# One of three shifted bit patterns on GpSimd, query rows and turned products by DMA, features by fours, in a one-core gated attention kernel

## The chip, the cores and the metric

The kernel runs on one core of a Trainium2 chip. The metric is the device time of one execution in microseconds (us); the median of the runs shown is the time of a version. A core has TensorE (PE in the profile, its weight loads are PEld), VectorE (DVE), ScalarE (ACT), GpSimd (POOL) and SyncE (SP, which here only issues DMAs). Each engine works through its own instructions in order and waits on semaphores.

## What is computed

Two attention blocks over the same x, mixed by a gate. S = 2048 rows, D = 512, 32 heads of 16.

```
x = A_x                                   # (1, 2048, 512) bfloat16
g = sigmoid((x * gate_w).sum(-1))
# A: softmax attention
q, k, v = split(x @ A_wqkv)               # 32 heads of 16
p = softmax(q k^T / 4);  a = (p v) @ A_wo
# B: linear attention with learned features
q, k, v = split(x @ B_wqkv)
phi(t) = [softmax(t w_phi), softmax(-t w_phi)]        # 32 features a head
o = phi(q) (phi(k)^T v) / (phi(q) sum(phi(k)) + 1e-6);  b = o @ B_wo
out = g * a + (1 - g) * b
```

## The kernel before, in words

**Branch A.** The queries go in four chunks of 512 columns, and in each the 32 heads as eight groups of four heads: 32 groups. A group takes 16 key tiles of 128 rows. One key tile of one group is a *pack*; there are 512 packs, and a pack has four *units* (one head, 128 keys, 512 queries). For a unit TensorE makes the scores in a row of 32 of its array (`_scores`, L814), an engine makes the exponential, and TensorE multiplies it with the values in a column of 32 (`_values`, L928), four heads side by side, adding up over the 16 key tiles in one PSUM bank of the group. A column of ones in the values gives the denominators.

Two engines make exponentials. *ScalarE* (`_exp`, L862) takes three units and two units in turn out of a ring of five PSUM banks. *VectorE* takes the packs that the table `AWAY` (L713) marks, 109 in all, at most five of a group's key tiles 1, 4, 7, 10, 13. It makes a linear bit pattern out of the scores (`_vector_bits`, L755, one operation for each unit, PSUM to SBUF, uint16), which read as bfloat16 is an exponential with straight lines between powers of two, and then three copies shifted by a constant (`_vector_terms`, L771, `SHIFTS`, up to two packs in one operation). TensorE adds all four patterns up by multiplying each with the values, two of them with values scaled by 0.75 (`vc`). So such a pack has 16 value matmuls and not 4.

`_norm` (L944) ends a group: a transpose in blocks of 32 from PSUM (n_t1, L949), the denominators times the gate's factor (n_den), a reciprocal (n_rec), a product (n_mul, L960), and for each second group a transpose back (n_back, L965), into `onTA`, from which the output matmuls read. `_proj_q` (L637) makes the queries of two groups: a projection, and one VectorE operation (L651) that writes them twice, times a mask, so that in each copy the other group's rows of 16 are zero.

**Branch B.** `_b_pair` (L1056) works on two tiles of 128 rows: a projection to the features' arguments (pq, L1069), its negative beside it (b_neg, L1086), a tree of maxima (b_max), the subtraction (b_sub, L1091), the exponential on ScalarE (b_exp, L1094), a tree of sums, reciprocals and products (`_b_scale`). Three slots of `bq` hold such pairs. For the keys `_b_kv` (L1125) multiplies the features with the values and adds the result to `kvacc` on VectorE; for the queries `_b_phit` turns them by a transposing DMA, and `_b_num` (L1182) makes the numerators, the denominators (nb_den, L1200), a reciprocal and a product (nb_mul, L1204). `_b_out` and `_out` multiply with the output weights, B and A into the same bank.

**The order.** Nothing is ordered by hand within an engine. Every operation is given to a planner (`Plan`) with an engine, a cost, its dependencies, a priority in packs ("due") and sometimes an earliest pack (`rel`). `Plan.order` goes through time and takes for each engine what is ready, the most urgent first; `emit` writes out one queue for each engine and the semaphores. Three PSUM banks beside the ring are given out as they come free. So that TensorE keeps busy, the planner sets filler matmuls by zero weights between (`_fill`, L935) and full matmuls ahead of scores (L835). Constants of `_Kernel` (L363 to L369, and L968) move whole kinds of operations: `BITS`, `STEP`, `LEAD`, `TERM`, `NORM`, `QDUE`, and `K0`, `SK`, `Q0`, `SQ` for branch B. All but a few DMAs are issued by SP, in planned order.

Of the kernel before, what the change touches and what calls it, by code (L numbers as in the profile page):

```python
# [10 lines left out]
P = 128  # L11
# [32 lines left out]
class Op:  # L44
    def __init__(self, eng, fn, cost, name, prio, rel, kind, lat):
# [17 lines left out]
        self.filled = 0  # L63

# [38 lines left out]
class Plan:  # L103
# [9 lines left out]

    def __init__(self):
        self.ops = []
        self.now = -1
        self.free_banks = []
        self.keep = None
        self.open = None
        self.pad = None  # L120

    def op(self, eng, fn, cost, reads=(), writes=(), deps=(), name="", prio=0.0, rel=-99, kind="full",
# [24 lines left out]
        o.array = cost if array is None else array  # L147
        self.ops.append(o)
# [7 lines left out]
    def order(self):  # L156
# [5 lines left out]
        for o in self.ops:  # L162
            if not o.left:
                avail[o.eng].append(o)
        free = dict.fromkeys(self.ENGS, 0.0)
# [5 lines left out]
        while left:  # L171
            best = None
            for e in self.ENGS:
                found, limit = [], 1e9
                for o in avail[e]:
# [8 lines left out]
                    if o.acquire is not None:  # L184
                        banks = self._bank_for(o)
                        if not banks:
                            continue
                        r = min(b[1] for b in banks)
                        if r > t:
                            t = r  # L190
                    o.ready = t
# [51 lines left out]
            free[e] = array.seq if e == "PE" else o.end  # L243
            queues[e].append(o)
# [113 lines left out]
class _Kernel:  # L358
# [5 lines left out]
    NB, LEAD = 4, 15.75  # L364
    FIRST = 13
    KT0, KTS, NKT = 1, 3, 5
    KEEP = 14
    TURN = 2.5
    STEP, BITS, TERM, PVX, NORM, QDUE, PUT = 0.55, -40.0, 4.0, -0.4, -6.0, -15.5, 8  # L369
# [28 lines left out]
    def _memory(self, ctx):  # L398
# [31 lines left out]
        self.qT = sb("qT", [P, self.NQS, QCH], BF16)  # L430
        self.ET = sb("ET", [P, self.NSLOT, QCH], BF16)
        self.T1 = sb("T1", [P, 2, 16, 32], F32)
        self.rinv = sb("rinv", [P, 2, 16], F32)
        self.T2 = sb("T2", [P, 16, 32], BF16)
        self.ghb = sb("ghb", [P, self.NT], F32)
# [4 lines left out]
        self.bq = sb("bq", [P, 3, 2, 2 * D], BF16)  # L440
        self.btree = sb("btree", [P, 32, 8, 4], BF16)
        self.bsum = sb("bsum", [P, P], F32)
        self.brec = sb("brec", [P, P], FP16)
# [8 lines left out]
        self.warm = self.bq[:, 2, 0, 0:QCH]  # L452
        self.wpp = self.bq[:, 2, 1, 0:4 * P].rearrange("p (c j) -> p c j", c=4)
        self.gwb = self.bq[:, 2, 0, QCH:2 * QCH].rearrange("p (c m) -> p c m", c=4)
# [107 lines left out]
    def _projections(self):  # L562
# [5 lines left out]
        self.b_onTA = [[B() for _ in range(4)] for _ in range(2)]  # L568
        self.b_T1, self.b_rinv, self.b_T2 = [B(), B()], B(), B()
        self._warm(9)  # L570
        for j in range(NQC):
            if j == 0:
                self._proj_k0(0, 2)
                self._proj_q(0, 0, 3)
                self._proj_k0(1, 4)
            else:
                self._proj_k(0, j)
# [51 lines left out]
    def _proj_k(self, cp, j):  # L629
        due = 32 * cp + 3 * j - 14.0 if cp else 4 * j - 2.0  # L630
# [6 lines left out]
    def _proj_q(self, qc, cp, bank=None):  # L637
        n = qc * 4 + cp
        due = 32 * n + self.QDUE if n else -2.0
# [3 lines left out]
        reads = [self.b_xT[qc], self.b_WA[0][cp > 0], self.b_mask]  # L643
        if n == 0:
            one = lambda side: lambda e, b: e.tensor_scalar(self.qT[:, s0 + side, :], b, self.mask[:, side:side + 1],
                                                            None, op0=ALU.mult)
            self._proj(lhs, rhs, reads, [one(0), one(1)], self.c_dve(512), due, due - 99, "qproj",
                       [self.b_qT[s0], self.b_qT[s0 + 1]], bank=bank)
            return
        self._proj(lhs, rhs, reads,  # L650
                   [lambda e, b: e.tensor_tensor(self.qT[:, s0:s0 + 2, :], b[:, None, :].to_broadcast([P, 2, QCH]),  # L651
                                                 self.mask[:, :, None].to_broadcast([P, 2, QCH]), ALU.mult)],
                   self.c_dve(1024), due, due - 10, "qproj", [self.b_qT[s0]])
        self.b_qT[s0 + 1] = self.b_qT[s0]

    def _proj_v(self, cp, j):
# [3 lines left out]
        due = 32 * cp + 4 * j - (6.5 if cp else 0.5)  # L660
# [15 lines left out]
    def _gate(self):  # L676
# [4 lines left out]
        z = self.bq[:, 0:2].rearrange("p s t j -> p (s t j)").bitcast(F32).rearrange("p (q b d) -> p q b d", q=NQC, d=32)  # L681
        for qc in range(NQC):
            job = Job()

            def mm(e, qc=qc, job=job):
# [4 lines left out]
            m = op("PE", mm, 4 * self.c_pe(512), reads=[self.b_xT[qc], b_gwb], name="gate", prio=18 + qc, rel=12,  # L690
                   acquire=job)
            last.append(op("DVE", lambda e, qc=qc, job=job: e.transpose(
                z[:, qc].rearrange("p b d -> p (b d)"), self._bank(job)), 0.74, deps=[m], name="gate_t", prio=18 + qc,
# [3 lines left out]
        for r, sign in ((0, -1.0), (1, 1.0)):  # L697
# [3 lines left out]
        self.gate_z = last[-2:]  # L701
# [5 lines left out]
        self.b_ghb.writers = [op("DVE", lambda e, i=i: e.tensor_copy(  # L707
            self.ghb[32 * i:32 * i + 32, :],
            self.gh[32 * i:32 * i + 32, 1].rearrange("p q (t i) -> p (q t) i", i=4)[:, :, i]), 0.1, reads=[self.b_g],
            name="gate_b", prio=26) for i in range(4)]  # L710


    AWAY = (4, 5, 23, 20, 5, 27, 30, 14, 27, 22, 15, 25, 13, 30, 7, 31, 27, 31, 18, 21, 23, 26, 27, 29, 15, 29, 11, 25, 15, 26, 29, 15)  # L713

    def _plan_vector(self):
# [16 lines left out]
        for n in range(1, 4 * self.NQC):  # L732
            self.hooks.setdefault(max(0, 32 * n - 30), []).insert(0, lambda n=n: self._proj_q(*divmod(n, 4)))
# [8 lines left out]
    def _vector_bits(self, pair, side, pack, due):  # L742

        op = self.plan.op
        tile, b = self.va[:, pair, side], self.b_va[pair][side]
        step = self.STEP
        parts = []
        for j in range(self.NB):
# [7 lines left out]
                tile[:, j, :], self._bank(job), SCALE * LOG2E * 128.0, (127.0 - LOG2_SUM) * 128.0,  # L756
                op0=ALU.mult, op1=ALU.add), self.c_dve(512), deps=[m] + b.readers, name="v_bits", prio=at + self.BITS,
                release=job))
        b.writers, b.readers = parts, []
        self.last_bits = parts  # L760

    def _vector_terms(self, pair, packs):
# [3 lines left out]
        for j, pack in enumerate(packs):  # L766
            self.terms[pack] = [(self.va[:, pair, j], self.b_va[pair][j], 0)]
        a, n = flat(self.va[:, pair]), size * self.NB * QCH
        for k, (shift, scaled) in enumerate(SHIFTS):
            t, b = self.vp[:, k], self.b_vp[k]  # L770
            self.plan.op("DVE", lambda e, t=t, shift=shift: e.tensor_scalar(flat(t), a, float(shift), None, op0=ALU.add),  # L771
                         0.07 + n * 0.00026, reads=self.b_va[pair][0:size], writes=[b], name="v_term",
                         prio=packs[0] + self.TERM)
            for j, pack in enumerate(packs):
                self.terms[pack].append((t[:, j], b, scaled))

    def _attention(self):
# [12 lines left out]
        self.b_va, self.b_vp = [[Buf(), Buf()] for _ in range(2)], [Buf() for _ in SHIFTS]  # L790
        self._value_copies()
# [78 lines left out]
    def _pv(self, p):  # L870
# [10 lines left out]
        for u in range(4 * p, 4 * p + 4):  # L881
            deps.append(self.exps[self.in_group[self.place[u]]])
            src[u % 4] = self.ET[:, self.place[u] % self.NSLOT, :]
# [26 lines left out]
    def _pv_terms(self, p):  # L910
# [3 lines left out]
        for tile, buf, scaled in self.terms.pop(p):  # L914
            src = {i: tile[:, i, :].bitcast(BF16) for i in range(4)}
            V = self.vc[:, g8 // 2, (kt - self.KT0) // self.KTS] if scaled else None
# [7 lines left out]
    def _values(self, e, ot, g8, kt, src, V=None):  # L924
        V = self.V[:, kt, g8 // 2] if V is None else V
        for i, tile in src.items():
            v0 = 17 * (2 * i + g8 % 2)
            ins = e.matmul(self._bank(ot)[32 * i:32 * i + 32, :], V[:, v0:v0 + 32], tile,  # L928
# [15 lines left out]
    def _norm(self, qc, src, side, last, dst, b_dst, due, job, alone=False):  # L944
# [19 lines left out]
        if side == 1:  # L964
            op("DVE", lambda e: e.transpose(dst, T2[:].rearrange("p b s -> p (b s)")), 0.63,  # L965
               reads=[b_T2], writes=[b_dst], name="n_back", prio=due)

    K0, SK, Q0, SQ = 28.0, 11.85, 206.0, 16.8  # L968

    def _branch_b(self):  # L970
        op, NT, NQC = self.plan.op, self.NT, self.NQC
        B = Buf
        self.b_bq = [B() for _ in range(3)]
        for b in self.b_bq[:2]:
            b.readers = list(self.gate_z)
        self.b_WT = B()
        self.b_WP = [B() for _ in range(2)]
        self.b_tree, self.b_bsum, self.b_brec = B(), B(), B()
# [6 lines left out]
        self.n_pair = 0  # L985
# [4 lines left out]
        self.b_bq[2].readers = self.b_gwb.readers + self.b_warm.readers + self.b_wphi.readers  # L990
        for t in range(0, NT, 2):
            due = self.K0 + self.SK * t
            self._b_v(t, due)
            self._b_v(t + 1, due + 1)
# [316 lines left out]
```

## Time and profile before

| | before |
|---|---|
| median of 3 runs (lowest to highest) | 780.46 us (779.11 to 780.57) |
| profiled execution, its own time | 787.43 us |
| its span, first to last instruction | 785.5 us |
| mean granted TensorE clock in it | 0.987 |
| exponentials of scores (L862), count | 645 |
| feature exponentials (L1094), count and mean | 16, 2027 ns |
| bit operations of VectorE (L755), count | 436 |
| issues on SP: transposing DMAs of features and of branch B's products | 16 and 16, 3.2 and 2.4 us to landing |

A row of the groups of instructions has the line, the engine, the operation, output and inputs with their shapes, the count, and then the busy time in us, the mean of one in ns, and how long the engine was idle just before such instructions and who ended it. VectorE's and ScalarE's records of neighbouring instructions overlap a little, so means times counts add up to more than busy time. A row of the waits has the waiting engine and line, the one that released it, the total in us, the times, and the longest.

### The profile page before, as it was taken

How to read it: one execution, taken by the hardware profiler on the slowest of the kernel's cores; microseconds unless marked ns; L12 is line 12 of the kernel's file. 1: busy time of each engine (PE TensorE's matmuls, PEld its weight loads, DVE VectorE, ACT ScalarE, POOL GpSimd, SP SyncE). 2: the span in 40 equal slices, each digit the busy share in tenths (PEclk: the TensorE clock that was granted, in tenths of full speed). 3: DMA queues.
4: the chain of work that ended last, by engine and by line, in shares of the span. 5: the costliest groups of instructions: out<-in, count | busy, mean ns of one | idle time of the engine just before them, and what ended most of it. 6: DMA issues, size and time to landing. Idle time of an engine off the chain costs nothing.

```text
span 785.5 us, 16524 instructions
## 1 busy us (share of the span) xinstructions
PE 753.5 (96%) x7224; PEld 234.9 (30%) x7294; DVE 713.1 (91%) x1178; ACT 762.1 (97%) x665; POOL 6.4 (1%) x16
## 2 busy tenths in 40 slices
PE   9999999999999999999999999999999999999998
PEld 3333333233212222222222232223222222222222
DVE  3779999998969999999999997998999999988994
ACT  6999999999969999999999999999999999999996
POOL 2000000000000000000000000000000000000000
PEclk9999999999959999999999999999999999999999
DMA  9200000000000000000101020010200102001010
GB/s 223 100 3 1 2 1 2 1 1 2 1 1 2 1 2 1 1 2 1 29 1 28 8 41 21 9 34 15 41 8 8 41 2 55 8 8 41 8 22 28
DMA packets 42183, 15.75 MB, mean 20 GB/s; under 512 B 36992, under 2 KB 41600, under 8 KB 42112
## 3 DMA queue, kind: packets, MB, share of 16 engines
q1 hardware_dynamic: 40240, 14.05, 8.1%
q8 instruction: 57, 0.93, 0.5%
q10 hardware_dynamic: 1872, 0.66, 0.4%
q14 instruction: 14, 0.11, 0.0%
HBM read 4.21 MB, written 2.10 MB: 8 GB/s over the span
## 4 chain that ended last, share of the span: by engine, by line
ACT 61%; PE 21%; DVE 16%; issue 1%; DMA 1%
ACT ET L862 59%; PE ps L814 7%; DVE va L755 7%; PE ps L928 6%; DVE vp L771 4%; PE ps L611 3%; ACT bq L1094 2%; PE ps L935 1%; PE ps L1221 1%; PE ps L665 1%; DMA xT<-in_A_x_dram 1%; PE ps L1254 1%; DVE T L949 1%; PE ps L835 1%; DVE bq L1069 0%
## 5 line engine op out<-in xcount | busy, mean ns | idle before, releaser
L862 ACT ACTIVATE ET<-ps 128x1536 bf16<-128x1536 f32 (+1 forms) x645 | 734.6, 1349 | 14.1 <-PE ps L814 13.2
L814 PE MATMUL ps<-qT,kT 32*128 32x512 bf16 x2048 | 342.0, 387 | 14.7 <-ACT ET L862 5.7
L755 DVE TENSOR_SCALAR va<-ps 128x512 uint16<-128x512 f32 x436 | 283.1, 680 | 18.0 <-PE ps L814 17.3
L771 DVE TENSOR_SCALAR vp<-va 128x4096 uint16<-128x4096 uint16 (+1 forms) x183 | 199.6, 1101 | 1.7 <-PE ps L928 1.2
L814 PEld LDWEIGHTS ps<-qT,kT 32*128 32x128 bf16 x2048 | 84.9, 91 | 276.4 <-ACT ET L862 153.0
L928 PE MATMUL ps<-ET,V 128*32 128x512 bf16 x1612 | 155.9, 390 | 0.3 <-DVE nb L1204 0.3
L928 PE MATMUL ps<-vp,vc 128*32 128x512 bf16 x872 | 75.8, 384 | 0.5 <-DVE vp L771 0.3
L935 PE MATMUL ps<-kT,zero 128*32 128x512 bf16 x784 | 70.9, 390 | 0.0
L928 PEld LDWEIGHTS ps<-ET,V 128*32 128x32 bf16 x1612 | 40.7, 95 | 69.7 <-issue 56.4
L611 PE MATMUL ps<-WB,xT 128*128 128x512 bf16 x167 | 50.6, 393 | 3.9 <-issue 2.4
L928 PE MATMUL ps<-va,V 128*32 128x512 bf16 x436 | 43.7, 391 | 0.0
L928 PE MATMUL ps<-vp,V 128*32 128x512 bf16 x436 | 42.2, 389 | 0.5 <-DVE vp L771 0.4
L611 PE MATMUL ps<-xT,WA 128*128 128x512 bf16 (+1 forms) x117 | 33.8, 381 | 2.4 <-issue 2.1
L1094 ACT ACTIVATE bq<-bq 128x2048 bf16<-128x2048 bf16 x16 | 32.4, 2027 | 0.0
L949 DVE STREAM_TRANSPOSE T<-ps 128x512 f32<-128x512 f32 x32 | 22.7, 710 | 7.8 <-PE ps L928 7.7
L928 PEld LDWEIGHTS ps<-vp,vc 128*32 128x32 bf16 x872 | 19.9, 95 | 31.9 <-issue 18.4
L1069 DVE CAST bq<-ps 128x512 bf16<-128x512 f32 x32 | 21.8, 683 | 5.8 <-PE ps L611 5.7
L935 PEld LDWEIGHTS ps<-kT,zero 128*32 128x32 bf16 x784 | 17.3, 94 | 31.9 <-issue 29.6
L665 PE MATMUL ps<-WA,xT 128*128 128x128 bf16 x256 | 20.6, 220 | 0.3 <-DVE WB L1043 0.3
L611 PEld LDWEIGHTS ps<-WB,xT 128*128 128x128 bf16 x192 | 13.0, 99 | 22.8 <-issue 13.2
L1091 DVE TENSOR_TENSOR bq<-bq,btree 128x2048 bf16<-128x2048 bf16 x16 | 19.4, 1215 | 0.1
L651 DVE TENSOR_TENSOR qT<-ps,mask 128x1024 bf16<-128x1024 f32 x15 | 18.2, 1212 | 1.4 <-PE ps L611 1.4
(80 smaller groups left out, 376.2 us busy)
## 6 DMA issues: line engine op xcount, KB each, us to landing
WB<-in_B_wqkv_dram SPq DMA_DIRECT2D x1, 1536.0 KB, 7.4
out_dram<-WB SPq DMA_DIRECT2D x12, 128.0 KB, 1.7
WA<-in_A_wqkv_dram SPq DMA_DIRECT2D x3, 384.0 KB, 4.9
WoA<-in_A_wo_dram SPq DMA_DIRECT2D x1, 512.0 KB, 8.4
WoB<-in_B_wo_dram SPq DMA_DIRECT2D x1, 512.0 KB, 9.0
WA<-in_A_wqkv_dram ACTq DMA_DIRECT2D x3, 128.0 KB, 4.1
phiT<-bq SPq DMA_TRANSPOSE x16, 3.2
WT<-nb SPq DMA_TRANSPOSE x16, 2.4
```

Of the source, the lines that this page charges most:

```text
L611: ins = e.matmul(self._bank(job)[:, 0:n], lhs(c), rhs(c), start=(c == 0), stop=(c == 3))
L665: ins = e.matmul(self._bank(job)[:, P * tt:P * tt + P], self.xT[:, c, QCH * j + TOK * tt:QCH * j + TOK * tt + TOK], self.WA[:, 2, c, P * c ...
L755: parts.append(op("DVE", lambda e, j=j, job=job: e.tensor_scalar(tile[:, j, :], self._bank(job), SCALE * LOG2E * 128.0, (127.0 - LOG2_SUM) ...
L771: self.plan.op("DVE", lambda e, t=t, shift=shift: e.tensor_scalar(flat(t), a, float(shift), None, op0=ALU.add), 0.07 + n * 0.00026, reads= ...
L814: return e.matmul(out, self.kT[32 * i:32 * i + 32, cp, kt * TOK:(kt + 1) * TOK], self.qT[32 * i:32 * i + 32, s, :], start=True, stop=True, ...
L862: o = plan.op("ACT", lambda e: e.activation(self.ET[:, a % NS:a % NS + n, :], self.ps[:, self._ring(a):self._ring(a) + n, :], ACT.Exp, sca ...
L928: ins = e.matmul(self._bank(ot)[32 * i:32 * i + 32, :], V[:, v0:v0 + 32], tile, start=(kt == 0), stop=(kt == self.NT - 1), tile_position=( ...
L935: ins = e.matmul(self._bank(ot)[32 * i:32 * i + 32, :], self.zero[:], self.kT[:, 0, 0:QCH], start=False, stop=False, tile_position=(0, 32 ...
L949: op("DVE", lambda e: e.transpose(T1[:, side].rearrange("p b s -> p (b s)"), src()), 0.635, deps=last, writes=[b_T1[side]], name="n_t1", p ...
L1069: [lambda e, b, k=k: e.tensor_copy(bq[:, k].rearrange("p (g s v) -> p g s v", g=8, s=2)[:, :, 0, :], b.rearrange("p (g v) -> p g v", g=8))],
L1091: + [("b_sub", two(2048), lambda e: e.tensor_tensor(x, x, spread(tree[:, :, 0]), ALU.subtract))],
L1094: op("ACT", lambda e: e.activation(flat, flat, ACT.Exp), self.c_act(2048) + 0.045, reads=[b], writes=[b], name="b_exp", prio=due + 1)
```

## The change, and its diff

- **Shifted patterns.** The first of the three (`BY_POOL = 0`) is made by GpSimd, one pack at a time. Such an operation, a *rider*, is bound to the first bit operation of the next pack: it waits for VectorE's operation just ahead of it in VectorE's queue, so that it runs beside the four bit operations. The planner keeps GpSimd's riders and VectorE's operations named in `SHARED` apart in time.
- **Packs.** `AWAY` marks 111 packs, other ones than before; many constants of the order move, `BITS`, `BURST` (for `STEP` within a pack) and `FIRST` among them.
- **Query rows.** VectorE copies the projection once (`qs`), and eight DMAs on SP put rows of 16 into the two copies of `qT`, whose other rows GpSimd clears at the start. The very first queries are projected in two halves of 256 columns and written by VectorE as before (`_proj_q0`).
- **Turned products.** n_back becomes 16 DMAs that place blocks of 32 by 32 (`turned`) and one transposing DMA, except for the last pair of groups.
- **Features by fours.** `_b_quad` takes four tiles; the negative is not made: maxima and minima are taken of the same argument, two subtractions write two sides, and ScalarE's exponential has the scale +1 or -1. Sums, reciprocals and products go over four tiles at once. `bq` holds one such set in place of three pairs. `kvacc` is added to once for four tiles.
- **Numerators.** The gate's factor goes from a product with the denominators into one fused operation (scalar_tensor_tensor).

The diff, cut to its core:

```diff
-    NB, LEAD = 4, 15.75
-    FIRST = 13
+    NB, LEAD = 4, 16.0
+    BURST, RIDE = 0.1, 2.5
+    FIRST = 5
-    KEEP = 14
+    KEEP = 13
+    GAP, KDUE, VDUE, GATE = 3.45, -16.25, -11.75, 14.0
-    STEP, BITS, TERM, PVX, NORM, QDUE, PUT = 0.55, -40.0, 4.0, -0.4, -6.0, -15.5, 8
+    BY_POOL = 0
+    STEP, BITS, TERM, PVX, NORM, QDUE, PUT = 0.625, -80, 5.5, 0.8, 2, -22.0, 3.8
...
-    K0, SK, Q0, SQ = 28.0, 11.85, 206.0, 16.8
+    K0, SK, Q0, SQ = 33.0, 12.25, 216.0, 16.0
...
+    SHARED = {"v_term", "b_max", "b_sub", "b_sum", "b_rec", "b_ratio", "b_mul", "n_den", "n_rec", "n_mul", "n_back",
+              "kvbd", "vcopy", "gate_h", "gate_b", "gate_z"}
...
+                    if o.port:
+                        t = max(t, port[other[e]])
...
+            for x in o.riders:
+
+                x.deps.extend(queues[e][-1:])
...
+    def _rider(self, eng="POOL"):
...
+        (pair, side, pack), k = self.riding, self.BY_POOL
+        shift, scaled = SHIFTS[k]
+        self.riding = None
+        b = self.b_vp[k][side]
+        o = self.plan.op(eng, lambda e: e.tensor_scalar(
+            self.vp[:, k, side], self.va[:, pair, side], float(shift), None, op0=ALU.add),
+            self.RIDE if eng == "POOL" else 0.07 + self.NB * QCH * 0.00026, reads=[self.b_va[pair][side]], writes=[b],
+            name="v_term", prio=pack + self.TERM)
+        o.port = True
...
         for k, (shift, scaled) in enumerate(SHIFTS):
...
+            if k == self.BY_POOL:
+                continue
...
+        tile = self.qs[:, n % 2]
+        self._proj(lhs, rhs, reads, [lambda e, b: e.tensor_copy(tile, b)], self.c_dve(512), due, due - 10, "qproj",
+                   [self.b_qs[n % 2]])
+        parts = [lambda e, r=r: e.dma_start(self.qT[r:r + DH, s0 + r // DH % 2, :], tile[r:r + DH, :])
+                 for r in range(0, P, DH)]
...
-        if side == 1:
+        if side == 1 and alone:
             op("DVE", lambda e: e.transpose(dst, T2[:].rearrange("p b s -> p (b s)")), 0.63,
                reads=[b_T2], writes=[b_dst], name="n_back", prio=due)
...
+        elif side == 1:
+            parts = [lambda e, i=i, x=x: e.dma_start(self.turned[32 * x:32 * x + 32, :, 32 * i:32 * i + 32],
+                                                     T2[32 * i:32 * i + 32, x:16:4, :])
+                     for i in range(4) for x in range(4)]
+            self.dma("SP", f"on{due:.0f}", parts, cost=0.55 * len(parts), reads=[b_T2], writes=[self.b_turned], prio=due,
+                     lat=3.0)
...
+        for side, out, alu in ((1, n, ALU.min), (0, p, ALU.max)):
+            t, buf = self.btree[:, side], (pos, neg)[side]
+            at = 6 - 2 * side
+            fold("b_max", 32, t, p, alu, at, [pos], tree[side])
+            run("b_sub", two(2048), lambda e, out=out, t=t: e.tensor_tensor(out, p, spread(t[:, :, 0], 32), ALU.subtract),
+                at, [pos, tree[side]], [buf])
+            op("ACT", lambda e, side=side: e.activation(sides[side], sides[side], ACT.Exp, scale=1.0 - 2 * side),
+               self.c_act(2048) + 0.045, reads=[buf], writes=[buf], name="b_exp", prio=due + gap * at + 1)
...
+            op("DVE", lambda e, hf=hf, sums=sums: e.reciprocal(rb[:, hf], sums()[:, :, 16]), 0.17,
+               deps=[m] + b_nb.writers, writes=[b_rb], name="nb_rec", prio=due)
+            parts.append(op("DVE", lambda e, hf=hf, sums=sums: e.scalar_tensor_tensor(
+                out=nb[:, 256 * hf:256 * hf + 256].rearrange("p (h d) -> p h d", d=16), in0=sums()[:, :, 0:16],
+                scalar=self.ghb[:, t:t + 1], in1=rb[:, hf, :, None].to_broadcast([P, 16, 16]), op0=ALU.mult,
```

## The prediction, made before the changed kernel had run

> **What bounds the kernel now.** I read the busy table first, then ScalarE's waits, then both ends of the timeline, then VectorE by form, then GpSimd.
>
> From the page, busy time, share of the span and instructions:
>
> ```profile
> PE 753.5 (96%) x7224; PEld 234.9 (30%) x7294; DVE 713.1 (91%) x1178; ACT 762.1 (97%) x665; POOL 6.4 (1%) x16
> ```
>
> Two engines are above 90% beside TensorE, whose busy figure is stretched by pipelining and by filler matmuls (L935, 784 of them). ScalarE is idle for only 785.5 - 762.1 = 23.4 us. Its whole list of waits, as total, times, longest:
>
> ```profile
> ACT ET L862 <- PE ps L814: 13.2, 7, 5.5
> ACT xT L1260 <- PE ps L1254: 4.2, 1, 4.2
> ACT L862 <- issue: 2.3, 1, 2.3
> ACT ET L862 <- PE ps L928: 0.3, 1, 0.3
> ```
>
> Two of them are the start (5.5 and 2.3), one is the end (4.2, and about 2.7 us more pass after its last instruction). Six waits of L814 remain, 13.2 - 5.5 = 7.7 us. Windows (PE, PEld, DVE, ACT, POOL busy, then the granted clock, DMA) put them in one place:
>
> ```profile
> 196.00:220.00 24.00, 22.38 (x204) 6.40 (x199) 22.36 (x36) 22.63 (x20) 0.00 (x0) 0.90 0.01 2
> 220.00:240.00 20.00, 19.67 (x117) 4.05 (x114) 13.57 (x24) 13.54 (x11) 0.00 (x0) 0.61 0.00 0
> 240.00:300.00 60.00, 57.63 (x599) 16.76 (x600) 58.08 (x88) 59.93 (x54) 0.00 (x0) 1.00 0.01 1
> 300.00:400.00 100.00, 96.25 (x934) 28.30 (x947) 99.88 (x164) 99.88 (x87) 0.00 (x0) 1.00 0.03 7
> ```
>
> From about 215 to 235 us TensorE had half its clock; outside that stretch ScalarE is never idle for long. The profiled execution took 787.43 us (span 785.5 and 1.93 around it). Without the 7.7 us it is 779.7; the runs shown lie at 779.11 to 780.57, median 780.46. So I take it that the timed runs had no such stretch, and that between its first exponential at 9.08 us and its last, which ends at 777.5, **ScalarE sets the time**. VectorE is full as well at 300 to 400 us, but ScalarE was not waiting for it there.
>
> **The change, part by part.**
>
> *Two more packs on VectorE (109 to 111).* ScalarE loses 8 of 1612 score units. The chain of waits has 50 exponentials in 56.51 us and 47 in 53.34, so one of three units and one of two take 2 x 1.13 = 2.26 us, 0.45 per unit: 8 x 0.45 = **-3.6 us on the path**. The feature exponentials stay sixteen of 2048 columns, with runs of 64 instead of one block; between nothing and the 0.1 us by which these sixteen differ among themselves, each, I take nothing. TensorE gets 24 more value matmuls, six sets of four at 0.22 us, 1.3 us, and VectorE 8 more bit operations. TensorE has cover: its score weight loads waited 153.0 us for ScalarE.
>
> *One of three shifted patterns to GpSimd.* The rows that VectorE shows:
>
> ```profile
> L755 DVE TENSOR_SCALAR va<-ps 128x512 uint16<-128x512 f32 x436 | 283.1, 680 | 18.0 <-PE ps L814 17.3
> L771 DVE TENSOR_SCALAR vp<-va 128x4096 uint16<-128x4096 uint16 x144 | 173.5, 1214 | 1.6 <-PE ps L928 1.2
> L771 DVE TENSOR_SCALAR vp<-va 128x2048 uint16<-128x2048 uint16 x39 | 26.2, 681 | 0.1
> ```
>
> 199.7 us over 327 patterns is 0.61 each. 222 remain: 135.5, so -64.2. GpSimd gets 111 of 2048 elements each. Its rows of before:
>
> ```profile
> L534 POOL MEMSET V<- 128x1024 bf16 x1 | 1.3, 1258 | 0.0
> L550 POOL TENSOR_TENSOR bq<-wphi,head 128x256 bf16<-128x256 bf16 x2 | 1.2, 612 | 12.8 <-DMA wphi<-in_B_w_phi_dram 12.8
> L679 POOL COPY bq<-gw 128x512 bf16<-128x512 bf16 x1 | 0.6, 609 | 0.4 <-DMA gw<-in_gate_w_dram 0.4
> ```
>
> By the copy 4 x 609 = 2.4 us, by the product of two inputs 8 x 612 = 4.9. One input and one output is nearest to the copy: I take 2.4, and keep 4.9. At 2.4 GpSimd is busy for 266 us. A rider starts when the VectorE operation ahead of the next pack's bit operations is done; four bit operations in a row take 2.45 us (at 214.28). So the rider just fits beside them, and its matmuls come several packs later, since bits are made 16 packs ahead.
>
> A rule bears on this: the Trainium skill, GPSIMD Engine Reference, section Engine selection, gives elementwise work on a tile to VectorE, but calls GpSimd about line rate for one input. By a line rate at its 1.2 GHz clock a rider would be an estimated 1.7 us; the copy's row says 2.4, and the sum stands by the row.
>
> *Query rows.* VectorE's product with the mask (15 x 1212) becomes a copy (683, the L1069 cast of the same shape): -7.9. SP gets 8 DMAs each time. An issue is between 0.22 us (the four of the gate weights took 0.87) and 0.47 (two stores took 0.93), a landing 1.7 to 4.2: 3.5 to 8 us. The due time moves from 15.5 to 22 packs ahead; a pack is 768 / 512 = 1.5 us, so 33 us cover them.
>
> *Turned products.* 15 of 16 turns of 696 leave: -10.4. In their place stand 16 DMAs and one transposing DMA: 3.5 to 7.5 us of issue, 1.7 to 4.2 to land, 2.4 for the turn (the row of nb): 8 to 14 us. Behind a waiting one on SP stand the query DMAs, the feature turns and the stores. In the last chunk the last pair that goes this way is normalised some 27 packs, 40 us, before the end; the last two groups still turn on VectorE. I cost both parts at nothing on the path. Without that cover the 8 to 14 us would stand in front of the output matmuls.
>
> *Features by fours.* No b_neg: -6.6. Sums in wider operations: 16 x (675 + 416 + 280 + 273) = 26.3 becomes 8 x about 2.72 = 21.7, -4.6. Reciprocals, ratio and product: -2.4. kvacc 16 to 8: -3.3. nb_den gone: -5.0; the fused nb_mul between its present 413 and 413 + 159, I take 413. A single bq means that the next four tiles wait for the kv matmuls of the last four: planned 41 packs behind the start, of a period of 49. What waits is a projection, and no exponential of the scores.
>
> *VectorE's sum:* -64.2 - 7.9 - 10.4 - 6.6 - 4.6 - 2.4 - 3.3 - 5.0 + 5.4 = -99; neighbouring records overlap by some 0.08 us and about 140 instructions go, so **about -88: 713 to 625 us**. It hides wholly behind ScalarE, and is worth nothing by itself.
>
> *Start.* The first 512 query columns come in two halves. Their eviction, 0.75 us at 7.84 just ahead of the first scores, becomes one of 256 (0.42); half of the matmuls may run before the second half of x lands. Between 0 and 0.8 us; I take **-0.4**. GpSimd's clearing of qT (2 x 1258) lies in its 12.8 us of waiting. The end is unchanged.
>
> Sum: 780.46 - 3.6 - 0.4 = **776.5 us**.
>
> **The rivals.**
>
> *1. The port (slower).* If GpSimd and a VectorE operation on SBUF data exclude each other, a rider that outlasts its four bit operations holds up sums, maxima and shifts behind it. No row of before has the two side by side. The place is 291 to 485 us, where VectorE was busy for 190.0 of 194 us. The change frees 194 / 785 x 88 = 22 there, with 4 idle: 26 us of room for some 27 riders. At 4.9 us each overhangs by 2.45. If half of them block, 33 us, 7 over: 784 us; if all, 66, 40 over: 816. It turns slower than before from 26 + 4 = 30 us of overhang on, 1.1 us for each of 27, a rider of 3.6 us. For it speaks the two-input row, against it the copy and the memset. The Trainium skill, SBUF — State Buffer, section Who interferes with whom, states such a lock, whole instructions long; no run here shows it yet.
>
> *2. The clock (slower).* A stretch at half clock, as at 215 to 235 us, in the timed runs: +7.7, 784.2 us. Ahead of it stood four bit operations in a row (214.28) and single score matmuls between them; bursts of bits are what the change makes the rule (BURST 0.1 for STEP 0.55). Against it: the fillers remain, and no timed run of before shows it. The Trainium skill, TensorE: Matmul & The Clock Gate, part 1 on the HAM clock gate, has the clock halved after an idle window; here TensorE was 94% busy by its records ahead of the drop, so busy records don't settle it.
>
> *3. The gain is eaten.* Small new waits of ScalarE for a late b_sub (16 times, 0.0 us now) or for scores behind a value matmul that waits for a rider: 3 to 4 us, 780 us, no change.
>
> *4. It doesn't do what it says:* riders that find no burst stay on VectorE (0.61 each); at 68 more, VectorE has 693 us, below the 713 of now: 776.5 all the same.
>
> **How the numbers follow.** The forecast 0.57, rival 4 0.05 at the same time, rival 3 0.11, rival 1 0.13, rival 2 0.14. This measurement can tell 0.2% (1.6 us) from no change. Faster is 0.57 + 0.05 = 0.62, same 0.11, slower 0.27. The range goes down to 780.46 - 3.6 - 0.8 and 1.7 us of small idle time (780.46 less the 778.7 that start, ScalarE's work and end add up to): 774.4; up to rival 2 and the lower price of rival 1: 784.5. Outside are rival 1's higher prices and any surprise below. The likeliest case's own range is 774.4 to 778.9.
>
> **What would show it.** ScalarE's busy time near 758.5 and its waits as now, without the stretch at half clock; VectorE near 625; 111 riders near 2.4 us with the bit operations at 0.6 us apart beside them; SP's DMAs landing tens of us before their readers. Wrong would be: waits of b_exp, value matmuls waiting for GpSimd, riders over 3.6 us, a granted clock below 1 in the middle.

## The result: 293 us slower, and the profile after

Median of 5 runs after the change: **1072.37 us** (1070.15 to 1074.62), beside 779.11 us of the kernel before (5 runs, 778.88 to 780.57). The ratio is 1.3747 [1.371, 1.3783]. The forecast was 776.5, its range ended at 784.5. Here and below a median is over all executions, while a ratio leaves out those more than 1.5% above the fastest of their kernel, one each in f1 and h1.

The page of the changed kernel, first the busy table and the row of the granted clock:

```profile
span 1071.7 us, 17019 instructions
...
PE 911.3 (85%) x7314; PEld 239.9 (22%) x7314; DVE 789.5 (74%) x1015; ACT 785.6 (73%) x662; POOL 601.1 (56%) x126
...
PEclk9997998978887788676787888868866777887678
```

ScalarE had 97% and has 73%, no engine is above 90% any more, and the clock, 9s in all slices but one before, is 6 to 8 in 34 of the 40. With no full engine, the time goes into waits of one engine for another. The groups name the link (line, engine, operation, output and inputs, count; busy us, mean ns; idle before):

```profile
L940 ACT ACTIVATE ET<-ps 128x1536 bf16<-128x1536 f32 (+1 forms) x642 | 755.3, 1246 | 267.6 <-PE ps L892 261.6
L827 POOL TENSOR_SCALAR vp<-va 128x2048 uint16<-128x2048 uint16 x109 | 592.6, 5437 | 439.9 <-PE ps L1009 111.9
```

A rider takes **5.44 us and not 2.4** (592.6 / 109). VectorE by form shows what it does to its neighbours:

```profile
L809 DVE TENSOR_SCALAR va<-ps 128x512 uint16<-128x512 f32 x444 | 293.0, 684 | 142.1 <-PE ps L892 140.3
L846 DVE TENSOR_SCALAR vp<-va 128x4096 uint16<-128x4096 uint16 x96 | 191.8, 2003 | 10.8 <-PE ps L1009 10.7
L846 DVE TENSOR_SCALAR vp<-va 128x2048 uint16<-128x2048 uint16 x30 | 37.5, 1255 | 3.9 <-PE ps L1009 3.7
```

The bit operations out of PSUM keep their 0.68 us. The shifts, SBUF to SBUF, which took 1214 and 681 ns before, take 2003 and 1255: their records contain the time in which they were held. The waits (engine and line, what released it, total us, times, longest):

```profile
ACT ET L940 <- PE ps L892: 261.6, 209, 6.7
...
PEld ps L1009 <- POOL vp L827: 111.4, 44, 6.5
...
PE ps L1009 <- POOL vp L827: 92.5, 35, 6.2
```

TensorE, in order, stands 35 times for 2.6 us on average before the value matmuls of a rider, and ScalarE's scores stand behind them. One such case in the timeline (start, us, engine, line; in brackets the idle time before and who ended it):

```profile
313.10 2.49 DVE L809 TENSOR_SCALAR va<-ps 128x512 uint16<-128x512 f32 x4
...
313.26 5.36 POOL L827 TENSOR_SCALAR vp<-va 128x2048 uint16<-128x2048 uint16 x1 [0.63 <-DVE vp L846]
...
315.51 1.47 DVE L1170 TENSOR_TENSOR btree<-btree 128x128 bf16<-128x128 bf16 x1
316.90 2.27 DVE L846 TENSOR_SCALAR vp<-va 128x2048 uint16<-128x2048 uint16 x1
...
318.68 0.62 PE L1009 MATMUL ps<-vp,V 128*32 128x512 bf16 x4 [3.27 <-POOL vp L827]
...
319.89 1.45 ACT L940 ACTIVATE ET<-ps 128x1536 bf16<-128x1536 f32 x1 [3.52 <-PE ps L892]
```

The rider lies beside the four bit operations as planned (313.10 to 315.59), but outlasts them by 3.0 us. In that overhang a maximum of 128 columns (0.22 us where nothing holds it) takes 1.47, and a shift of 2048 (0.68) takes 2.27 and ends 0.55 us after the rider. TensorE waits 3.27 us for the rider and ScalarE 3.52 for scores. That one engine holds up the other, and that results come late, are here in one picture; the experiments take them apart.

### The profile page after: what moved, and what is told of

It is laid out like the page before. It is cut to its first block, busy times and chain, and to the rows that moved or that the text cites. A ratio compares the mean times of both kernels' runs of the same rounds, so it can differ in the third digit from the quotient of the medians.

```text
span 1071.7 us, 17019 instructions
## 1 busy us (share of the span) xinstructions
PE 911.3 (85%) x7314; PEld 239.9 (22%) x7314; DVE 789.5 (74%) x1015; ACT 785.6 (73%) x662; POOL 601.1 (56%) x126
## 4 chain that ended last, share of the span: by engine, by line
PE 51%; DVE 22%; POOL 19%; ACT 3%; issue 3%; POOLq 1%; DMA 0%; DVEq 0%
POOL vp L827 19%; PE ps L892 19%; PE ps L1009 17%; DVE vp L846 9%; PE ps L642 6%; PE ps L1016 4%; DVE va L809 4%; ACT ET L940 3%; DVE btree L1170 2%; PE ps L1311 1%; PE ps L715 1%; PE ps L1344 1%; DVE bq L1152 1%; DVE T L1041 1%; DVE btree L1188 1%
## 5 line engine op out<-in xcount | busy, mean ns | idle before, releaser
L940 ACT ACTIVATE ET<-ps 128x1536 bf16<-128x1536 f32 (+1 forms) x642 | 755.3, 1246 | 267.6 <-PE ps L892 261.6
L827 POOL TENSOR_SCALAR vp<-va 128x2048 uint16<-128x2048 uint16 x109 | 592.6, 5437 | 439.9 <-PE ps L1009 111.9
L892 PE MATMUL ps<-qT,kT 32*128 32x512 bf16 x2048 | 392.4, 450 | 34.7 <-DVE vp L846 12.3
L846 DVE TENSOR_SCALAR vp<-va 128x4096 uint16<-128x4096 uint16 (+1 forms) x126 | 228.9, 1825 | 14.8 <-PE ps L1009 14.4
L1009 PE MATMUL ps<-ET,V 128*32 128x512 bf16 x1604 | 184.1, 462 | 1.0 <-DVE T L1030 0.9
L1009 PE MATMUL ps<-vp,vc 128*32 128x512 bf16 x888 | 96.0, 454 | 12.4 <-DVE vp L846 12.2
L1016 PE MATMUL ps<-kT,zero 128*32 128x512 bf16 x800 | 90.2, 478 | 0.0
L642 PE MATMUL ps<-WB,xT 128*128 128x512 bf16 x192 | 63.5, 432 | 4.1 <-DVE VB L1139 1.8
L1009 PEld LDWEIGHTS ps<-vp,V 128*32 128x32 bf16 x444 | 12.1, 101 | 123.7 <-POOL vp L827 111.4
L1170 DVE TENSOR_TENSOR btree<-btree 128x512 bf16<-128x512 bf16 (+2 forms) x48 | 30.6, 664 | 0.0
```

What stands on the lines that cost most here:

```text
L642: ins = e.matmul(self._bank(job)[:, 0:n], lhs(c), rhs(c), start=(c == 0), stop=(c == 3))
L827: o = self.plan.op(eng, lambda e: e.tensor_scalar(self.vp[:, k, side], self.va[:, pair, side], float(shift), None, op0=ALU.add), self.RIDE ...
L846: self.plan.op("DVE", lambda e, k=k, shift=shift: e.tensor_scalar(flat(self.vp[:, k]), flat(self.va[:, pair]), float(shift), None, op0=ALU ...
L892: return e.matmul(out, self.kT[32 * i:32 * i + 32, cp, kt * TOK:(kt + 1) * TOK], self.qT[32 * i:32 * i + 32, s, :], start=True, stop=True, ...
L940: o = plan.op("ACT", lambda e: e.activation(self.ET[:, a % NS:a % NS + n, :], self.ps[:, self._ring(a):self._ring(a) + n, :], ACT.Exp, sca ...
L1016: ins = e.matmul(self._bank(ot)[32 * i:32 * i + 32, :], self.zero[:], self.kT[:, 0, 0:QCH], start=False, stop=False, tile_position=(0, 32 ...
```

## The experiments

Theories at the start: (A) riders hold VectorE's operations on SBUF (the port, rival 1); (B) the riders are only slow, and TensorE waits for their results; (C) the other parts cost, DMAs above all; (D) the clock is a loss of its own (rival 2). Each edited kernel is planned anew, so neighbours differ a little in their order as well.

**e1: riders on VectorE, all other parts of the change kept.**

```diff
-        rider = self._rider()
+        if self.riding is not None:
+            self._rider("DVE")
+        rider = None
```

> The changed kernel with all 111 riders made by VectorE again (one operation of 2048 elements each, near 0.68 us); everything else of the change stays: query rows and turned products by DMA, features by fours, 111 packs, the new order. Theory (the rider on GpSimd is the whole cause; in the trace it takes 5.36 us and not 2.4): VectorE near 625 + 68 = 693 us, ScalarE full, the forecast's 775 to 785 us. Rival (the DMAs, the fours or the new order carry a part of their own): above 820 us, with waits of ScalarE that no rider explains.

Measured 801.36 us, ratio 1.0267 [1.0243, 1.0291], between the 785 of the theory and the 820 of the rival: the rider is most of the loss, not all. The riders' place on GpSimd is 271 of the 293 us; 22 us have another cause. The busy table of this kernel:

```profile
PE 758.6 (95%) x7116; PEld 233.8 (29%) x7183; DVE 699.1 (87%) x1124; ACT 762.4 (95%) x662; POOL 8.6 (1%) x17
```

**e2, e3: riders of 64 and of 1024 elements in place of 2048.** The columns left out are cleared once.

```diff
-            self.vp[:, k, side], self.va[:, pair, side], float(shift), None, op0=ALU.add),
+            self.vp[:, k, side, 0:2], self.va[:, pair, side, 0:2], float(shift), None, op0=ALU.add),
```

(e3; in e2 `0, 0:64`.)

> The changed kernel's order, waits and dependencies to the instruction, but a rider works on 64 of its 2048 columns (near 0.3 us); so most of the first shifted pattern is left out of the result. Theory (the rider's duration is the cause): 774 to 785 us, clock near 1. Rival (the order itself, or its waits and semaphores on GpSimd, cost what is lost): above 850 us.

> As the one with short riders, but 1024 of 2048 columns, so half of the first shifted pattern is left out: by 5.36 us for 2048 near 2.7 us, about the price that the prediction took for a whole rider. Theory (duration against the four bit operations of 2.45 us decides): 775 to 800 us, VectorE's operations on SBUF held up by 0.3 us at most. Rival (the exclusion of the two engines costs at any length): above 850 us.

Measured 796.15, ratio 1.022 [1.0201, 1.0239], with riders of 0.44 us, and 793.46, ratio 1.0186 [1.0167, 1.0204]. That is in e3's range; e2's ended at 785 and left no room for the 22 us of e1. In e3:

```profile
L827 POOL TENSOR_SCALAR vp<-va 128x1024 uint16<-128x1024 uint16 x109 | 310.3, 2847 | 441.8 <-PE ps L1012 102.6 <-DVE vp L846 94.1 <-DVE bq L1155 51.2
L846 DVE TENSOR_SCALAR vp<-va 128x4096 uint16<-128x4096 uint16 x96 | 123.6, 1293 | 2.7 <-PE ps L1012 2.6
```

At 2.85 us, 0.36 over the four bit operations, shifts are held for 79 ns on average, and nothing is lost against riders of 0.44 us. So no fixed cost for each rider is seen (e1, without riders on GpSimd, took longer than both); the loss sets in somewhere between 2.85 and 5.44 us.

**e4: whole riders that nobody waits for.** They work in place on their own tile, in a chain of their own; TensorE multiplies a fixed tile in their stead, so that pattern's values are left out.

```diff
+                if id(o) not in rider and o not in self.alone:
+                    o.deps = [d for d in o.deps if id(d) not in rider]
...
-            self.vp[:, k, side], self.va[:, pair, side], float(shift), None, op0=ALU.add),
+            self.vp[:, k, side], self.vp[:, k, side] if eng == 'POOL' else self.va[:, pair, side],
...
+            if buf in self.b_vp[self.BY_POOL]:
+                src = {i: lambda: self.kT[:, 0, 0:QCH] for i in range(4)}
```

> The changed kernel's order with riders of full length (2048 columns, on GpSimd's own tile, in place), started as before by VectorE's queue but in a chain of their own: no engine waits for one, and TensorE multiplies a fixed tile in place of the first shifted pattern, which is so left out of the result. It keeps GpSimd's use of SBUF beside VectorE and takes away the waits for its results. If the waits for late results are most of the loss: 780 to 850 us. If the exclusion of VectorE's operations on SBUF is most of it (in the trace they are about 140 us longer in all): above 900 us.

Measured 999.24, ratio 1.2827 [1.2799, 1.2855]. Forms and waits of this kernel:

```profile
L859 DVE TENSOR_SCALAR vp<-va 128x4096 uint16<-128x4096 uint16 x96 | 203.7, 2128 | 2.9 <-PE ps L1026 2.8
```

```profile
ACT ET L955 <- PE ps L907: 191.7, 164, 5.9
```

Against e2, 999.2 - 796.2 = **203 us** come with holding alone, no result being waited for; the remaining 1072.4 - 999.2 = 73 us are gone with the waits for results. Both theories hold, A with the larger part. (The two need not add up strictly: a late rider is partly late because it was itself behind something. Each part includes what TensorE's lower clock adds, which was 0.977 in e2, 0.847 in e4 and 0.806 with whole riders.)

**f4: the operations by themselves.** A program with none of the kernel's work, GpSimd first alone, then beside one VectorE operation at a time.

```diff
+        add = lambda e, o, i: e.tensor_scalar(o[:], i[:], 30.0, None, op0=ALU.add)
+        ints = lambda e: e.tensor_tensor(i32(ub), i32(ua), one[:].bitcast(I32).to_broadcast([P, 1024]), ALU.add)
```

> No attention at all: the output is filled with a constant. GpSimd makes operations of 2048 elements alone (uint16 plus constant, half of it, bfloat16 plus constant, float32 plus constant, two copies, 1024 integers of 32 bits, a memset), and then uint16 and integer riders beside four bit operations from PSUM, beside one shift of 4096 on VectorE, and beside a maximum of 1024. Theory: uint16 plus constant takes 5.4 us alone, so nothing in the attention kernel slows it; the copies near 2.4; the integers near 2.5; the bit operations are not held up, the shift and the maximum begin only when the rider has ended. Rival: alone it takes near 2.4 us and VectorE doubles it.

Its timeline: alone; then a rider beside four bit operations, beside a shift and beside a maximum of two inputs; last, an addition of integers beside the same maximum:

```profile
33.10 5.37 POOL L30 TENSOR_SCALAR ub<-ua 128x2048 uint16<-128x2048 uint16 x1
38.55 2.77 POOL L34 TENSOR_SCALAR ub<-ua 128x1024 uint16<-128x1024 uint16 x1
41.40 5.37 POOL L30 TENSOR_SCALAR bb<-ba 128x2048 bf16<-128x2048 bf16 x1
46.85 5.37 POOL L30 TENSOR_SCALAR fb<-fa 128x2048 f32<-128x2048 f32 x1
52.28 1.89 POOL L37 COPY ub<-ua 128x2048 uint16<-128x2048 uint16 x1
...
56.21 1.89 POOL L31 TENSOR_TENSOR ub<-ua,one 128x1024 int32<-128x1024 int32 x1
...
60.94 5.37 POOL L30 TENSOR_SCALAR ub<-ua 128x2048 uint16<-128x2048 uint16 x1 [0.97 <-DVE ot L83]
61.53 2.48 DVE L44 TENSOR_SCALAR bits<-ps 128x512 uint16<-128x512 f32 x4
...
73.57 5.37 POOL L30 TENSOR_SCALAR ub<-ua 128x2048 uint16<-128x2048 uint16 x1 [0.95 <-DVE ot L83]
74.17 5.84 DVE L46 TENSOR_SCALAR vb<-va 128x4096 uint16<-128x4096 uint16 x1
...
88.22 5.37 POOL L30 TENSOR_SCALAR ub<-ua 128x2048 uint16<-128x2048 uint16 x1 [1.96 <-DVE ot L83]
88.82 3.58 DVE L47 TENSOR_TENSOR tc<-ta,tb 128x1024 bf16<-128x1024 bf16 x1
...
116.46 1.89 POOL L31 TENSOR_TENSOR ub<-ua,one 128x1024 int32<-128x1024 int32 x1 [1.95 <-DVE ot L83]
117.08 1.82 DVE L47 TENSOR_TENSOR tc<-ta,tb 128x1024 bf16<-128x1024 bf16 x1
```

An addition of a scalar takes 5.37 us in all three types, with nothing beside it: the 2.4 us failed for the operation, not for contention. The copy of as many elements takes 1.89, less than the 2.4 that its row before had suggested. Beside a rider the bit operations out of PSUM are not held (2.48). A shift of 4096 that needs 1.21 us ends 1.07 us after the rider: it starts about when the rider ends. The maximum (0.68 where free) was expected to wait as long, but ends 1.2 us before the rider's record does, so it is let in earlier. Beside the addition of integers it is not: there it ends 0.55 us after it.

**f1: riders as additions of 32-bit integers**, two patterns of 16 bits in one element, 1.89 us alone.

```diff
+        o = self.plan.op(eng, (lambda e: e.tensor_tensor(
+            pairs(self.vp[:, k, side]), pairs(self.va[:, pair, side]),
+            self.shift[:].bitcast(dt.int32).to_broadcast([P, self.NB * QCH // 2]), ALU.add)) if eng == "POOL" else lambda e: e.tensor_scalar(
```

> The changed kernel's order and waits, riders on GpSimd and complete, but a rider adds two 16-bit patterns at a time: 1024 integers of 32 bits plus one constant (30 in each half), two inputs. By the row of before for two inputs, 612 ns for 256, a rider is near 2.5 us. Theory (a rider's length decides, whatever it computes): as with half riders, 785 to 800 us. Rival (only riders of one input go beside VectorE, or 32 bits are slower still): above 850 us.

Measured 798.35, ratio 1.0201 [1.0129, 1.0273]. Riders take 1.93 us in the kernel and all 2048 patterns are made: with a rider that fits, GpSimd is about as good a place as VectorE (e1, 1.0267; the intervals overlap), and VectorE falls from 699.1 to 650.1 us, which by itself brings nothing, since ScalarE sets the time. What is left, 2%, looks like the part that e1 has as well: TensorE waits for query rows four times, 5.2 us in all.

**f2, f3, h2: more filler matmuls** (in e1's, f1's and the changed kernel), to test theory D.

```diff
-    SPAN, SHARE, FILL = 3.0, 0.6, 0.2133
+    SPAN, SHARE, FILL = 3.0, 0.75, 0.2133
```

> All riders on VectorE as in the first experiment (801 us), and the planner's share of filler matmuls raised from 0.6 to 0.75. Theory (what is left of the loss there is TensorE's clock, halved for 3.4 to 13.7 us at a time where matmuls are sparse): the stretches at half clock go, granted clock 0.99 or more, 775 to 782 us. Rival (ScalarE's waits come from the order itself and the clock falls because of them): 795 us or more, as fillers only add work to TensorE.

> Integer riders on GpSimd and the share of filler matmuls 0.75. If both theories hold: the forecast's mechanism without its two flaws, 774 to 781 us, at least as fast as before. If the clock is not what is left: 790 us or more.

> The changed kernel, riders of 5.4 us on GpSimd and all else, with the share of filler matmuls 0.75 in place of 0.6. It asks how much of the 293 us is TensorE's clock (granted 0.81 on the mean). If the low clock only follows from TensorE's waits and costs little, since TensorE is waiting anyway: 1050 to 1090 us. If it is a loss of its own on top of the held-up operations: below 1000 us with a granted clock above 0.95. The fillers themselves cost time (801 to 843 us with riders on VectorE).

Measured 842.92, ratio 1.0799 [1.0742, 1.0857]; 843.47, 1.0813 [1.0746, 1.088]; and 1097.83, 1.4088 [1.4059, 1.4116]. The forecasts of f2 and f3 fell, and h2 ended just above the range for a clock that costs little. In f2 the clock is back (0.998, from 0.972), but TensorE is now the full engine (97%) and ScalarE waits 24.0 us for scores and 25.0 for value matmuls. In h2 the clock rises from 0.806 to 0.871 and the time too. So this way of keeping the clock costs more than it gives, and theory D is not shown as a loss that could be taken back by itself; what the halved clock adds to holds and waits in the changed kernel was not separated.

**Where the 22 us are.** In e1, TensorE stops in three places for something that stands behind the turned products on SP, and ScalarE after it. Two of them in the timeline, SP's queue and TensorE:

```profile
128.62 10.78 SPq L1051 DMA_DIRECT2D turned<-T  x16
139.45 6.05 SPq L678 DMA_DIRECT2D qT<-qs  x8
...
146.73 0.39 PE L894 MATMUL ps<-qT,kT 32*128 32x512 bf16 x1 [1.38 <-DMA qT<-qs]
...
420.36 10.95 SPq L1051 DMA_DIRECT2D turned<-T  x16
431.35 1.27 SPq L1265 DMA_TRANSPOSE WT<-nb  x1
...
434.48 1.42 PE L894 MATMUL ps<-qT,kT 32*128 32x512 bf16 x5 [2.17 <-DVE nb L1295]
```

Sixteen issues take 10.8 us, 0.67 each, and in front of TensorE stand the query rows in one case, in the other the turn of branch B's products (VectorE's nb_mul waited 2.01 us for it). TensorE stops for 1.4 and 2.2 us; the third stop, 2.42 us at 735.03, is for query rows again. Then the windows (length, PE, PEld, DVE, ACT, POOL busy, clock, DMA):

```profile
120.00:147.00 27.00, 24.61 (x251) 8.23 (x250) 22.08 (x35) 27.00 (x24) 0.00 (x0) 1.00 0.08 13
147.00:161.00 14.00, 13.78 (x86) 3.68 (x87) 6.73 (x10) 8.49 (x9) 0.00 (x0) 0.51 0.03 7
161.00:175.00 14.00, 13.76 (x117) 4.44 (x116) 10.25 (x16) 13.99 (x13) 0.00 (x0) 1.00 0.01 1
```

A stop of 1.4 us is followed by 13.7 us at half clock, in which ScalarE loses 14.0 - 8.5 = 5.5 us. After the other two stops it is the same, and with a fourth, short stretch (584 to 587 us) e1 has 44 us at half clock. In them and the stops ScalarE is idle for 18.8 us, about what separates e1 from g1 below. e1's own executions agree: the one with a clock of 0.981 had an estimated 15 us less at half clock (clock times span) than one with 0.972, and took 797.31 us and not 803.62. That is rival 2's loss, with a cause it did not name.

A stop is not all that it takes, though. At 391.19 us of the same trace TensorE stopped for 2.54 us (L915 waits for ScalarE) and the clock stayed at 1.00; and in the 12 us ahead of the half clock of the kernel before (203 to 215 us), TensorE was idle for only 0.9 us in all. What decides is open.

**g1: e1 with the turned products back on VectorE; g3: with the query rows back too; g4: f1 with the turned products back.**

```diff
-        if side == 1 and alone:
+        if side == 1:
...
-        elif side == 1:
-            parts = [lambda e, i=i, x=x: e.dma_start(self.turned[32 * x:32 * x + 32, :, 32 * i:32 * i + 32],
...
```

> All riders on VectorE (801 us in the first experiment), and the turned products undone: VectorE transposes them back as before the change, so 240 small DMAs and 15 transposing ones leave SP's queue. In the trace of the first experiment an issue of them takes 0.69 us, sixteen in a row 11 us, the query rows are issued behind them, and TensorE waits for the query rows 1.4 to 2.7 us, three times, with its clock halved from there on. Theory (SP's queue makes the query rows late, TensorE stops, the clock falls): no wait for query rows, granted clock 0.99 or more, 775 to 783 us. Rival (the order or the features by fours make the sparse stretches): 790 us or more.

> All riders on VectorE, turned products and query rows both by VectorE as before the change; what is left of it are the features by fours, the 111 packs, the fused numerators, the start in halves and the new order. VectorE then has about 693 + 10 + 8 = 711 us, as much as before. Theory (SP's queue is all that is left of the loss): 775 to 783 us, as with the turns alone. Rival (fours or order): 790 us or more.

> Integer riders on GpSimd (1.93 us each in the trace, 798 us in all) and the turned products by VectorE again. VectorE near 640 us. Theory (the two flaws are the rider's length and SP's queue): 774 to 781 us, no wait for query rows, granted clock 0.99 or more; possibly below both kernels. Rival: 790 us or more.

Measured 782.09, ratio 1.0029 [1.0004, 1.0054]; 787.86, 1.0101 [1.0077, 1.0126]; 788.22, 1.0116 [1.0048, 1.0184]. g1 takes back 19 of the 22 us as expected; g3 and g4 miss their theory's ranges by 5 and 7 us. In g1 the long waits are gone, and of the half clock 3.4 us are left:

```profile
PE 758.6 (97%) x7322; PEld 235.0 (30%) x7322; DVE 705.1 (90%) x1139; ACT 759.5 (97%) x662; POOL 8.1 (1%) x17
```

```profile
ACT ET L942 <- PE ps L894: 7.1, 7, 4.9
```

(4.9 of the 7.1 are the start.) The query rows by DMA do no harm when the 16 issues are not ahead of them: g3, without them, is slower than g1, with 7.6 us of waits for value matmuls (L1008) in a VectorE of 712.0 us. In g4 the integer riders are slower than VectorE's own by 6 us; stops of TensorE of 1.45 and 1.13 us behind shifts held to 2.92 us precede two of its three stretches at half clock. None of these beats the kernel before.

**g2, h1: the turned DMAs kept, but planned at 0.70 us an issue, or issued by GpSimd's queue** (both with e1's riders).

```diff
-            self.dma("SP", f"on{due:.0f}", parts, cost=0.55 * len(parts), reads=[b_T2], writes=[self.b_turned], prio=due,
+            self.dma("POOL", f"on{due:.0f}", parts, cost=0.55 * len(parts), reads=[b_T2], writes=[self.b_turned], prio=due,
```

(h1; in g2 `cost=0.7` here and at the query rows.)

> All riders on VectorE, all DMAs kept, but the planner counts 0.70 us for each issue of a small DMA instead of 0.55. Only the order changes. Theory (the planner let TensorE come to scores before their query rows had landed, since it took the issues for shorter): fewer or no waits for query rows, 776 to 792 us. Rival (the number of DMAs on the queue is too much whatever is planned): as the first experiment, 797 to 804 us.

> All riders on VectorE, all DMAs of the change kept, but the sixteen small DMAs of each turned product are issued by GpSimd, which has nothing else to do in this version, and not by SP (801 us with them on SP, 782 us with the turns back on VectorE). Theory (what costs is the place in SP's queue, where query rows and the numerators' turns stand behind sixteen issues of 0.69 us): no waits of TensorE for query rows nor of VectorE for the numerators' turn, 779 to 787 us. Rival (the number of small DMAs, or the late products themselves, cost what was lost): 795 us or more.

g2 measured 804.81, ratio 1.0313 [1.0227, 1.04]: its expectation fell. No query rows are late, but the new order has other stops, with 30.7 us at half clock around 390 to 421 us and 10.8 us of waiting at the end (two executions at a clock of 0.995 still took 800 us); so it says nothing on the issues. h1 measured 787.36, ratio 1.009 [1.0065, 1.0115]: 14 of the 19 us go with the place in SP's queue, just outside the theory's range. Its trace shows where the remaining 5 lie: in two stretches at half clock that g1 does not have. From 255 to 264 and from 385 to 401 us (clock 0.65 and 0.57) ScalarE is idle for 5.8 us. Ahead of the second, TensorE waited 2.54 us for ScalarE at 386.22, as it did in e1 at 391, this time with the clock falling; the first stands behind a wait of 0.80 us for a shift. None of these is a wait for a DMA. So these 5 us may belong to the order and not to the DMAs.

## Why the prediction was wrong, point by point

**The step that failed first:** "One input and one output is nearest to the copy: I take 2.4, and keep 4.9." Measured 5.36 to 5.44 us in the kernel and 5.37 alone, above even the upper bound. Nearness was taken by the number of inputs; but none of the three rows was an addition of a scalar, and the operation's kind decided. The Trainium skill (GPSIMD Engine Reference, section Engine selection) calls one input "roughly line-rate". The estimate of 1.7 us from that fits the copy (1.89 us for 2048) and is off by three for this operation; the measurement decides. The holds and the late results follow from it: at 2.4 us the step "the rider just fits beside them" would have been right, as riders of 1.93 (f1) and 2.85 us (e3) show. Whether it is the form with a scalar or its arithmetic that takes so long, no run separates.

**Rival 1 was the right mechanism at a wrong price.** Its rule (the Trainium skill, SBUF — State Buffer, section Who interferes with whom: the second to issue fully blocks until the first is through) agrees with the shifts of f4 (5.84 us beside a rider), but not with the maximum, which was let in before the rider's end. Rival 1 put its point of decision at riders of 3.6 us, and 2.85 (nothing lost) and 5.44 (276 us lost against e2) lie on its two sides. But it ended at 816 us. Three things were not in it. The rider was longer still, an overhang of 3.0 us for 2.45. It counted some 27 riders of one busy stretch, as if elsewhere VectorE's idle time would absorb the holds; yet a held VectorE stops what needs it at once, since TensorE works in order: e4 loses 203 us with VectorE at 80%. And it left out that results come late (73 us). It is also hard to see an order that hides it (an estimate; none was tried): riders and shifts exclude each other by f4, and 593 + 136 = 729 us of them (the shifts by form in g1) nearly fill the 776 us of the forecast; the two-input operations, 93 us in g1, are at least partly shut out too.

**The second step that failed:** "I cost both parts at nothing on the path." The issue was taken at 0.22 to 0.47 us and took 0.67; landing (1.8 us) was inside its bounds. The 8 to 14 us were asked about only as work of their own; what stood behind them on SP was named, "the query DMAs, the feature turns and the stores", but not followed to its readers. With the half clocks behind the stops the turned products cost 19 us, 14 of it by their place in the queue.

**Rival 2** came mostly behind stops of TensorE, and not by bursts of bits alone, which f2 and g1 have too, at a clock of 0.998. Its price fits the kernel before: of its 43 executions beside the experiments, three at a clock of 0.987 took 787.3 to 787.6 us, the others 778.6 to 781.1.

**Right:** that ScalarE sets the time, once riders and turned products are away (97% in g1); the bit operations' 2.45 us; the start, -0.4 (first exponential at 8.49 us in g1 for 9.08; in the changed kernel itself 9.02); nb_mul within its bounds (472 ns); VectorE's sum nearly, 625 (641.6 in e2 with riders of 64 elements; 693 with riders on VectorE, 699.1 in e1).

**The gain of two more packs**, -3.6, was -2.6 (ScalarE's busy time 762.1 to 759.5 in g1). And it was eaten: in g1 ScalarE is idle for 779.6 - 759.5 = 20.1 us, before for 23.4 - 7.7 = 15.7 outside its stretch at half clock. The end took about 0.9 us more, the start 0.6 less, so some 4 us are new small waits, rival 3's size; the views name 3.7 of them (2.2 for scores, 1.5 for value matmuls), 0.8 of them in g1's one stretch at half clock (479 to 483 us), and not why the others arose.

So the 293 us are: 271 the riders on GpSimd (some 200 by holds, 73 by late results), 19 the turned products, 3 the rest, the halved clock included in each.

## What to carry to other kernels

Price work that moves to another engine by a row of the same kind of instruction, or measure it first; rows that share shape or number of inputs can be off by a factor of two to three. Where engines exclude each other, count what the held operation's readers lose and not only the room of the held engine: an in-order TensorE passes each stop on. And a DMA's price is not its landing but its issues times what stands behind them in that queue, followed to the first reader that can be late.

## What the runs showed of the hardware

- GpSimd: 2048 elements a partition take 5.37 us as an addition of a scalar (uint16, bf16 or f32), 1.89 as a copy; an addition of 1024 integers of 32 bits with a broadcast constant, the same bytes as the first, takes 1.89.
- The hold is not the same for all: beside a rider of 5.37 us a shift waits for its end, a maximum of two SBUF inputs is let in earlier (it ends 1.2 us before the rider's record), an operation out of PSUM is not held. Beside an addition of integers of 1.89 us the maximum, too, waits for the end (f4).
- Half clock came for multiples of 3.41 us: once that in g1, 13.7 in e1, 30.7 in g2. In e1 three stops of TensorE of 1.4 to 2.4 us were followed by it, with its records 91% busy from 120 to 147 us ahead of the first; a stop of 2.54 us was not, and the 20.5 us of the kernel before came after 12 us with 0.9 us of idle time in all. The Trainium skill (TensorE: Matmul & The Clock Gate, part 1 on the HAM clock gate) names an idle window of about 3.4 us; these stops were shorter than one.
